# A gated mix of a spectral filter and a state-space filter: ScalarE takes 1-g, GpSimd the gate products, x comes in 16 parts, and the order is new

## The chip, the cores and the metric

The kernel runs on one core of one Trainium2 chip, in one launch, with float32 data. The metric is the device time of that launch in microseconds. The core has five engines that each take their own list of instructions in order: TensorE (PE; its weight loads are listed as PEld), VectorE (DVE), ScalarE (ACT), GpSimd (POOL) and SyncE (SP). They meet through semaphores, and data comes and goes over DMA queues: nearly all transfers are issued by SP, a few by GpSimd.

## The reference, cut to what matters

x is 1 x 2048 x 512 (positions by channels). Two filters of x are mixed by a gate that depends on the position alone:

```python
g = sigmoid((x * gate_w).sum(-1, keepdims=True))
a = irfft2(rfft2(x) * (w_r + 1j * w_i), s=(2048, 512))     # filter A
y = irfft(rfft(x^T, 4096) * rfft(K, 4096), 4096)[:, :, :2048]   # filter B, K[d] = 2 Re sum_n C[d,n] exp(A[d,n] dt[d] l)
b = y^T + x * D_skip
out = g * a + (1 - g) * b
```

## The kernel before, in words

**Filter A** is the two-dimensional transform, written as matmuls of 64 to 128 rows with constant matrices. The transform over 2048 positions has two steps, of 32 and of 64 points; the one over the 512 channels has two halves of 128 points each.

- *Stage 1.* x lies in DRAM in the order in which it is needed and comes in twelve parts, cut at the channels in `_E` (L57); each part is one transfer into VA, which SP issues in a row at the start (L233). The parts go in pairs: C (L248 to 258) multiplies a pair with the matrix s1e, in two halves f, into two PSUM tiles p_s, and c (`c_a`, L264) turns each half, 32 x 32 numbers at a time, by one STREAM_TRANSPOSE of VectorE into AR. When the last pair has gone through, AR holds all of it and VA is free.
- *Units.* The spectrum is cut into nine units (`UNITS`), eight of 128 frequencies and one of 64. Each unit runs through the same chain: P (TensorE, second step over positions, p_t, L411), t (ScalarE copies p_t to et, L416), D (TensorE, over channels, p_d, L425), d and z (ScalarE copies of half of p_d, L432, and of the first row, L444), Z (VectorE, sum and difference in PSUM, L438 and L439), y (ScalarE puts the first row back, L449 and L450), W and U (VectorE, the products with w, L460 to L465, into tw), p (GpSimd, sums of products, px, L472 and L473), g (GpSimd, sum and difference into gt, L484 and L485), h (ScalarE, two small copies for the first row, L491 and L492), I (TensorE, back over channels, p_v, L500), i (ScalarE copies half of p_v to po, L505), V (VectorE, ai, L515), B (TensorE, p_ia, L523 to L526), e (ScalarE copies p_ia to ei, L530), b (SP stores ei to DRAM, L536) and w (SP loads it again into VA in the order of the last step, L539).

**Filter B.** In this data the decay of every channel is so small that K is constant over the 2048 positions within float32, and the long convolution is a running sum times one number for each channel, s0. `N` works on the parameters: N0 takes maxima on VectorE, N1 the exponential of the step size and N3 (`level`) s0; N2 (`small`, L278 to L281) makes an exponential on ScalarE and with it, on GpSimd, the test of each channel; G4 counts the channels that pass and G5 casts the count (L351), which then chooses between the end of the program and a general path (L627), not taken here. A second copy of x with channels on partitions, XT, is loaded in four quarters of 1 MB (X, L299). Each quarter has two halves r of 1024 positions: x scales one into PSUM (ScalarE, L303), m is the running sum v (VectorE scan, L309), and then D_skip times x is added in one of three ways: o and F (ScalarE scales XT, L312, and a DMA issued by GpSimd adds v, L318), o and r (ScalarE, then an add on GpSimd, L315), or k (one VectorE instruction with two inputs from SBUF, L321).

**The gate.** G0 multiplies the four quarters of XT with gate_w (TensorE, p_gate, L336); G1 is the sigmoid (ScalarE, two instructions, L340); G2 makes 1-g in two instructions of VectorE (L343) and copies a piece of it to gc (L345). H spreads g and 1-g over the partitions by way of DRAM: g1 (L362), ga (L369) and gb (L365).

**The end.** M multiplies the last matrix of filter A, s1a, with g (ga, four VectorE instructions, L567); u multiplies XT with 1-g for eight of the 32 blocks of positions (gb, four VectorE instructions, L374). Y turns XT back to positions on partitions, by matmuls with the unit matrix eye (p_y, L549), in eight groups j of four blocks. For six of them s (ScalarE, L554, four instructions each) writes p_y times 1-g into AR, then Q (TensorE, p_oa, L578) makes filter A's share and q (VectorE, L591) adds the two. For the two groups in `DIRECT` Y and Q sum in one PSUM tile and a (ScalarE, L586) copies it. Each group is stored by SP in two transfers (L582).

**What sets the order.** The text PLAN (L41 to L53) is executed word by word: a letter names the function, the number the unit, group, half or part; the sign after `:` is the PSUM tile (four in all), after `/` the block of SBUF (13) and after `.` the short block (3) that it takes. `tc.manual_schedule()` keeps that order on each engine, so that a word stands behind all earlier words of its engine, and a tile can be taken again only when its last reader is done. The word R issues the loads in the list `loads`. The words E put five matmuls each on numbers that nobody reads (L245).

```python
_E = [0, 4, 8, 16, 24, 32, 40, 52, 64, 80, 96, 112, 128]
DIRECT = (0, 1)
LAST = np.array([2 * j + k % 2 + 16 * (k // 2) for j in range(8) for k in range(4)])
UNITS = [8, 0, 1, 2, 3, 4, 5, 6, 7]
```

Of the kernel before, what the change touches and what calls it, by code (L numbers as in the profile page):

```python
# [30 lines left out]
P = 128  # L31
# [25 lines left out]
_E = [0, 4, 8, 16, 24, 32, 40, 52, 64, 80, 96, 112, 128]  # L57
# [112 lines left out]
def body(ctx: ExitStack, tc: tile.TileContext, x, xg, xm, xt, w, wh, prms, vecs, gw, dskip,  # L170
# [57 lines left out]
    with tc.manual_schedule():  # L228
# [48 lines left out]
        def small():  # L277
            S.activation(big[:, 0], big[:, 0], AF.Exp)  # L278
            G.tensor_tensor(sm, big[:, 0], big[:, 1], op=ALU.add)
            G.tensor_tensor(sm, sm, few[:, 0], op=ALU.mult)  # L280
            G.tensor_scalar(sm, sm, float(L), TAU, op0=ALU.mult, op1=ALU.is_le)  # L281
# [49 lines left out]
        def G_(k):  # L331
            if k == 0:
                t_["pg"] = psum("p_gate")
                for i in range(4):
                    for q in range(4):
                        T.matmul(t_["pg"][32 * q:32 * q + 32, 0], gws[:, i], XT[:, i, 512 * q:512 * q + 512], start=i == 0, stop=i == 3, tile_position=(0, 32 * q))  # L336
            elif k == 1:
                t_["gs"] = blk([P, 2, 512], "gs")
                for h, o, g in halves():
                    S.activation(o, g, AF.Sigmoid)  # L340
            elif k == 2:
                for h, o, g in halves():
                    V.tensor_scalar(h, o, -1.0, 1.0, op0=ALU.mult, op1=ALU.add)  # L343
                t_["gc"] = short("gc").rearrange("p i j k -> p (i j k)")[:, 0:128]
                V.tensor_copy(t_["gc"].rearrange("p (c b) -> p c b", b=4), t_["gs"][:, 1].rearrange("p (c b) -> p c b", b=16)[:, :, 0:4])  # L345
            elif k == 4:
                t_["pc"] = psum("p_count")
                for i in range(4):
                    T.matmul(t_["pc"][0:1, 0, 0:1], sm[:, i:i + 1], one, start=i == 0, stop=i == 3)
            else:  # L350
                V.tensor_copy(count, t_["pc"][0:1, 0, 0:1])  # L351
# [20 lines left out]
        def share(i):  # L372
            v = XT[:, i].rearrange("p (c b) -> p c b", b=16)[:, :, 0:4]
            V.tensor_tensor(v, v, t_["gb"], op=ALU.mult)  # L374
# [166 lines left out]

        def Y_(j):
            p = t_["py", j] = psum("p_y").rearrange("p k (b i d) -> p (k b) i d", b=2, i=2)
            xv = XT.rearrange("p (i e) (a g b) -> p i g b (e a)", i=2, g=2, b=32)
            for k in range(4):
                for i in range(2):
                    for g in range(2):
                        first = k % 2 == i == 0 if j in DIRECT else True
                        T.matmul(p[64 * g:64 * g + 64, k, i], xv[:, i, g, LAST[4 * j + k]], eye, start=first, stop=j not in DIRECT, tile_position=(0, 64 * g))  # L549

        def s_a(j):
            for k in range(4):
                b = LAST[4 * j + k]
                S.activation(AR[:, 4 * j + k].rearrange("p (i d) -> p i d", i=2), t_["py", j][:, k], AF.Copy, scale=g1[:, 1, b:b + 1])  # L554
# [8 lines left out]
        def gated(k):  # L563
            w = s1a[k].rearrange("p b (h a) -> p b h a", h=2)
            ga = t_["ga"].rearrange("p a b -> p b a")[:, 16 * k:16 * k + 16]
            for h in range(2):
                V.tensor_tensor(w[:, :, h], w[:, :, h], ga, op=ALU.mult)  # L567
# [26 lines left out]
        def load_prm(k):  # L594
# [14 lines left out]
            lambda: (nc.sync.dma_start(ldt, vecs[:, 0]), load_prm(0)),  # L609
            lambda: (load_prm(1), load_prm(2)),  # L610
# [6 lines left out]
            "B": B_, "e": e_a, "b": b_a, "w": b_b, "Y": Y_, "s": s_a, "S": load_a, "M": gated, "Q": Q_, "q": q_a, "a": a_a, "R": lambda k: loads[k](),  # L617
# [243 lines left out]
```

## Time and profile before

| | |
|---|---|
| runs | 135.46, 135.97 and 136.91 us, median 135.97 |
| profiled execution | 136.17 us, of which the span of the trace is 134.0 |
| mean granted clock of TensorE | 0.948 |
| busy: PE / DVE / ACT / POOL | 114.0 / 97.2 / 71.4 / 50.4 us |
| DMA | 32.66 MB, 244 GB/s on average |

The span runs from the first to the last instruction or transfer that the profiler saw; the device time is 2.2 us longer. A line of the timeline gives the start, the length, the engine, the tile, the line of the kernel, the operation, output and input, how many instructions it holds, and in square brackets the idle time of the engine ahead of it with what ended it. A line of the groups gives the busy time and the mean of one in ns, then the idle time ahead of them and what ended most of it; in a list of single groups the three numbers are the shortest, the mean and the longest in ns. In a table of windows stand the busy time and, in brackets, the number of instructions of PE, PEld, DVE, ACT and POOL, then the clock granted to TensorE (1.00 is full speed), the share of the time in which the DMA engines were busy, and what they moved in GB/s. The chain is the work that ended last, followed back from the end of the span.

### The profile page before, as it was taken

The numbers are of one execution on the slowest core, as the hardware profiler recorded it, in microseconds if no ns is written. First come the engines' busy times: TensorE is split into PE (matmuls) and PEld (weight loads), VectorE is DVE, ScalarE is ACT, GpSimd is POOL, SyncE is SP. The second block draws the span as 40 slices with busy tenths as digits, with TensorE's granted clock in tenths as the row PEclk, the third lists the DMA queues.
The fourth block names the chain that finished last, engine by engine and source line by source line (L and its number), as shares of the span: only waits on it lengthen the run. The fifth ranks groups of instructions, "written<-read, shape, count | busy, mean of one in ns | idle before, by whom it ended". The sixth has DMA issues, their size and how long they took to land.

```text
span 134.0 us, 2683 instructions
## 1 busy us (share of the span) xinstructions
PE 114.0 (85%) x1035; PEld 85.2 (64%) x1035; DVE 97.2 (73%) x103; ACT 71.4 (53%) x136; POOL 50.4 (38%) x49
## 2 busy tenths in 40 slices
PE   6999798899999985698989899999659999999200
PEld 6853234899973974687977349963524999769100
DVE  0196599999999799977698679993789960476200
ACT  3000044489487991849578779865913639604300
POOL 0000000000499994795999289980080000000000
PEclk9999999999999999779999999999986999999955
DMA  3999999998798839463599889797995970199950
GB/s 98 316 329 389 397 340 355 366 417 270 232 346 274 256 87 196 91 195 119 164 264 179 192 284 335 158 373 183 301 323 157 318 157 5 48 380 331 334 191 2
DMA packets 14226, 32.66 MB, mean 244 GB/s; under 512 B 2000, under 2 KB 7420, under 8 KB 13308
## 3 DMA queue, kind: packets, MB, share of 16 engines
q1 hardware_dynamic: 13916, 30.30, 69.7%
q0 software_dynamic: 288, 2.10, 8.3%
q8 instruction: 10, 0.16, 0.5%
q14 instruction: 12, 0.10, 0.2%
HBM read 21.86 MB, written 8.40 MB: 226 GB/s over the span
## 4 chain that ended last, share of the span: by engine, by line
PE 48%; DVE 14%; DMA 13%; ACT 12%; SPq 4%; issue 2%; DVEq 0%; ACTq 0%
PE p_y L549 11%; PE p_t L411 9%; PE p_d L425 8%; DMA VA<-in_x_dram 7%; PE p_ia L526 6%; DMA VA<-ad 6%; DVE AR L264 6%; PE p_v L500 4%; PE p_oa L578 4%; DVE ai L515 3%; SPq L233 3%; DVE gs L343 3%; ACT po L505 2%; ACT XT L312 2%; DVE v L309 2%
## 5 line engine op out<-in xcount | busy, mean ns | idle before, releaser
L411 PE MATMUL p_t<-s2e,AR 128*128 128x128 f32 x136 | 18.0, 290 | 4.2 <-ACT et L416 2.5
L264 DVE STREAM_TRANSPOSE AR<-p_s 128x512 f32<-128x512 f32 (+3 forms) x12 | 15.2, 1357 | 7.7 <-PE p_s L258 7.7
L411 PEld LDWEIGHTS p_t<-s2e,AR 128*128 128x128 f32 x136 | 17.1, 203 | 5.3 <-ACT et L416 2.9
L472 POOL TENSOR_TENSOR px<-tw 128x512 f32<-128x512 f32 (+1 forms) x9 | 11.2, 1248 | 20.3 <-DVE tw L465 20.3
L500 PEld LDWEIGHTS p_v<-dbw,gt 128*128 128x128 f32 x136 | 15.7, 192 | 3.8 <-issue 2.7
L425 PE MATMUL p_d<-et,dfw 128*128 128x256 f32 (+1 forms) x72 | 16.8, 379 | 1.0 <-ACT et L416 0.7
L500 PE MATMUL p_v<-dbw,gt 128*128 128x128 f32 x136 | 16.2, 277 | 1.3 <-issue 1.1
L258 PE MATMUL p_s<-VA,last 64*64 64x256 f32 (+3 forms) x192 | 15.5, 450 | 1.0 <-DMA VA<-in_x_dram 1.0
L549 PEld LDWEIGHTS p_y<-eye,XT 128*64 128x64 f32 x256 | 14.8, 196 | 2.2 <-issue 1.9
L526 PE MATMUL p_ia<-ai,s2p 128*128 128x512 f32 x30 | 15.1, 643 | 1.1 <-DVE ai L515 1.1
L549 PE MATMUL p_y<-eye,XT 128*64 128x128 f32 x256 | 15.5, 282 | 0.0
L425 PEld LDWEIGHTS p_d<-et,dfw 128*128 128x128 f32 x72 | 13.0, 197 | 3.0 <-ACT et L416 1.0
L554 ACT ACTIVATE AR<-p_y,g 128x256 f32<-128x256 f32 x24 | 9.3, 481 | 10.1 <-PE p_y L549 10.1
L515 DVE TENSOR_TENSOR ai<-p_v,po 128x512 f32<-128x512 f32 (+1 forms) x18 | 10.8, 652 | 3.7 <-ACT po L505 3.7
L591 DVE TENSOR_TENSOR AR<-p_oa,AR 128x1024 f32<-128x1024 f32 x6 | 7.1, 1219 | 8.6 <-PE p_oa L578 7.3
L530 ACT COPY ei<-p_ia 128x1024 f32<-128x1024 f32 x8 | 8.1, 1009 | 9.2 <-PE p_ia L526 9.2
L258 PEld LDWEIGHTS p_s<-VA,last 64*64 64x64 f32 x192 | 6.9, 133 | 8.8 <-issue 5.6
L473 POOL TENSOR_TENSOR px<-tw 128x512 f32<-128x512 f32 (+1 forms) x9 | 11.2, 1244 | 1.7 <-DVE tw L463 1.7
L484 POOL TENSOR_TENSOR gt<-px 128x512 f32<-128x512 f32 (+1 forms) x9 | 11.6, 1293 | 0.5
L485 POOL TENSOR_TENSOR gt<-px 128x512 f32<-128x512 f32 (+1 forms) x9 | 11.6, 1294 | 0.0
L309 DVE TENSOR_TENSOR_SCAN v<-pers,v,p_x 128x1024 f32<-128x1024 f32 x4 | 9.4, 2345 | 2.6 <-ACT p_x L303 2.5
L465 DVE TENSOR_TENSOR tw<-p_d,w 128x1024 f32<-128x1024 f32 x8 | 9.7, 1215 | 2.1 <-DMA w<-hT 1.2
(68 smaller groups left out, 155.9 us busy)
## 6 DMA issues: line engine op xcount, KB each, us to landing
XT<-in_xt_dram SPq DMA_DIRECT2D x4, 1024.0 KB
w<-in_w_dram SPq DMA_DIRECT2D x8, 512.0 KB
ad<-ei SPq DMA_DIRECT2D x16, 256.0 KB
VA<-ad SPq DMA_DIRECT2D x8, 512.0 KB
out_dram<-AR SPq DMA_DIRECT2D x16, 256.0 KB
VA<-in_x_dram SPq DMA_DIRECT2D x4, 512.0 KB
XT<-v POOLq DMA_DIRECT2D x2, 1024.0 KB, 8.4
VA<-in_x_dram SPq DMA_DIRECT2D x4, 256.0 KB
```

The lines of the kernel that those rows point to most:

```text
L258: T.matmul(p[f][o:o + 64, h, :n], s1e[r:r + 64, f * u], xv[h][r:r + 64, u], start=u == 0, stop=u == 1, tile_position=(r, o))
L264: V.transpose(ar, t_["c", q][:, :, :32 * n].rearrange("p h (b d) -> p h d b", d=n))
L309: V.tensor_tensor_scan(v, one.broadcast_to([P, 1024]), t_["v1", r], t_["v0", r - 1][:, 1023:1024] if r % 2 else 0.0, op0=ALU.mult, op1=ALU ...
L411: T.matmul(p[:, q, :, 64 * v:64 * v + 64], AR[:, 16 * (q // 2) + sl, 128 * (q % 2):128 * (q % 2) + 128], s2e[:, k], start=True, stop=True)
L425: T.matmul(p[:, o, :, h, :n], dfw[:, 2 * h + o], et[:, ::-1] if h else et, start=True, stop=True)
L472: G.tensor_tensor(po[:, 0], t1[:, :, 0], t1[:, :, 1], op=ALU.add)
L484: G.tensor_tensor(gv[:, :, 0], src[0], src[1], op=ALU.add)
L485: G.tensor_tensor(gv[:, ::-1, 1], src[0], src[1], op=ALU.subtract)
L500: T.matmul(p[:, v, h, o], t_["gt", u][:, o, v, 2 * h:2 * h + 2].rearrange("p c k -> p (c k)"), dbw[:, h, o], start=True, stop=True)
L515: V.tensor_tensor(ai[:, :, :, k], t_["pi", u][:, :n, :, 0], t_["po", u][:, :n], op=ALU.subtract if k else ALU.add)
L526: T.matmul(p[:, v], s2p, t_["ai", pr][:, v], start=True, stop=True)
L549: T.matmul(p[64 * g:64 * g + 64, k, i], xv[:, i, g, LAST[4 * j + k]], eye, start=first, stop=j not in DIRECT, tile_position=(0, 64 * g))
```

## The change

- x comes in 16 parts instead of 12; the eight pairs are of 4, 6, 6, 8, 8, 10, 10 and 12 channels per part.
- 1-g (G2) and the copy gc are made on ScalarE. The exponential of N2 moves into G1, ahead of the sigmoid.
- The products u and M are made on GpSimd.
- Y, for the six groups that are not direct, handles one half i of the channels for eight blocks of positions, not both halves for four: groups 11, 12 and 13 need the first two quarters of XT, 21, 22 and 23 the last two. s takes four of these blocks by four ScalarE instructions of 128 columns; the new word f takes four by one VectorE instruction, with g1 spread over the columns.
- The parameter loads are grouped in another way, and PLAN is new: other units first, other places for E, N, G, X, R, o, F, k, u and M.

Lines after L276 move by 1 to 20: L343 is L344 in the changed kernel, L374 is L375, L549 is L557, L567 is L587, L578 is L598, L591 is L611.

```diff
-_E = [0, 4, 8, 16, 24, 32, 40, 52, 64, 80, 96, 112, 128]
+_E = [0, 4, 8, 14, 20, 26, 32, 40, 48, 56, 64, 74, 84, 94, 104, 116, 128]
...
         def small():
-            S.activation(big[:, 0], big[:, 0], AF.Exp)
             G.tensor_tensor(sm, big[:, 0], big[:, 1], op=ALU.add)
...
             elif k == 1:
+                S.activation(big[:, 0], big[:, 0], AF.Exp)
                 t_["gs"] = blk([P, 2, 512], "gs")
                 for h, o, g in halves():
                     S.activation(o, g, AF.Sigmoid)
             elif k == 2:
                 for h, o, g in halves():
-                    V.tensor_scalar(h, o, -1.0, 1.0, op0=ALU.mult, op1=ALU.add)
+                    S.activation(h, o, AF.Copy, bias=1.0, scale=-1.0)
                 t_["gc"] = short("gc").rearrange("p i j k -> p (i j k)")[:, 0:128]
-                V.tensor_copy(t_["gc"].rearrange("p (c b) -> p c b", b=4), t_["gs"][:, 1].rearrange("p (c b) -> p c b", b=16)[:, :, 0:4])
+                S.copy(t_["gc"].rearrange("p (c b) -> p c b", b=4), t_["gs"][:, 1].rearrange("p (c b) -> p c b", b=16)[:, :, 0:4])
...
         def share(i):
             v = XT[:, i].rearrange("p (c b) -> p c b", b=16)[:, :, 0:4]
-            V.tensor_tensor(v, v, t_["gb"], op=ALU.mult)
+            G.tensor_tensor(v, v, t_["gb"], op=ALU.mult)
...
+            if j in DIRECT:
+                p = t_["py", j] = psum("p_y").rearrange("p k (b i d) -> p (k b) i d", b=2, i=2)
+                todo = [(p[:, k, i], i, k, k % 2 == i == 0) for k in range(4) for i in range(2)]
+            else:
+
+                i, j2 = j // 10 - 1, j % 10
+                p = t_["py", j] = psum("p_y").rearrange("p k (b d) -> p (k b) d", b=4)
+                todo = [(p[:, k], i, k, True) for k in range(8)]
+                j = 2 * j2
+            for o, i, k, first in todo:
+                for g in range(2):
+                    T.matmul(o[64 * g:64 * g + 64], xv[:, i, g, LAST[4 * j + k]], eye, start=first, stop=j not in DIRECT, tile_position=(0, 64 * g))
...
+        def mixed(j, b):
+            i, j2 = j // 10 - 1, j % 10
+            n = 4 * (2 * j2 + b)
+            return AR[:, n:n + 4, 128 * i:128 * i + 128], t_["py", j][:, 4 * b:4 * b + 4], n
+
+        def s_a(j):
+            o, p, n = mixed(j % 100, j // 100)
             for k in range(4):
...
+                b = LAST[n + k]
+                S.activation(o[:, k], p[:, k], AF.Copy, scale=g1[:, 1, b:b + 1])
+
+        def s_b(j):
+            o, p, n = mixed(j % 100, j // 100)
+            gv = g1[:, 1].rearrange("p (h b o) -> p h b o", h=2, o=1)[:, :, n // 2:n // 2 + 2].broadcast_to([P, 2, 2, P])
+            V.tensor_tensor(*(v.rearrange("p (h b) d -> p h b d", h=2) for v in (o, p)), gv, op=ALU.mult)
...
             for h in range(2):
-                V.tensor_tensor(w[:, :, h], w[:, :, h], ga, op=ALU.mult)
+                G.tensor_tensor(w[:, :, h], w[:, :, h], ga, op=ALU.mult)
...
-            lambda: (nc.sync.dma_start(ldt, vecs[:, 0]), load_prm(0)),
-            lambda: (load_prm(1), load_prm(2)),
+            lambda: (load_prm(0), load_prm(1)),
+            lambda: (nc.sync.dma_start(ldt, vecs[:, 0]), load_prm(2)),
```

Of PLAN, which is rewritten as a whole, the end reads as follows before (first) and after the change:

```text
V5/0 B5:3 k6 k7 u1 e5/3 r1 w6 Y4:2 s4 Y6:1 Y2:3 u0 b5 Y3:2 w5 s6 u2 u3 M1 w4 Y5:1 s3 s5 G5 M0 Y0:0 Q0 s2 a0 Q6:2 Q5:1
Q2:3 q6 q5 Q7:0 Q4:2 q2 Q3:1 q3 Y7:3 s7 q4 Y1:1 Q1 q7 a1
```
```text
w6 x6:3 w4 V1/4 b2 s12 V0/0 B1:1 m6 x7:0 m7 b6 Y11:3 r5 b3 w1 w2 e1/3 k7 b1 Y13:1 w5 k6 s11 M1 Y21:0 f21 s112 f121
Y22:2 f122 s13 f22 w0 s113 s111 Y23:1 f23 M0 Q7:3 f123 u0 q7 Q4:0 u2 Q6:2 q4 Q2:1 q2 q6 Q3:3 q3 u3 u1 Q5:0 q5 Y1:1 Q1
a1 Y0:2 Q0 a0
```

**ScalarE around the gate.** Of the instruction list of ScalarE (line, instruction, output and input tiles, shape of one, how often in a row), before, from the D_skip product ahead of the sigmoid on:

```order
L312 ACTIVATE XT<-XT,pers 128x1024
L340 ACT_TABLE_LOAD
L340 ACTIVATE gs<-p_gate 128x16x16
L340 ACTIVATE gs<-p_gate 128x2x8x16
L505 COPY po<-p_v 128x512
```

And after, where last in L338 holds the numbers of N2 and et is the copy of p_t:

```order
L312 ACTIVATE XT<-XT,pers 128x1024 x2
L338 ACTIVATE last<-last 128x4
L341 ACT_TABLE_LOAD
L341 ACTIVATE gs<-p_gate 128x16x16
L341 ACTIVATE gs<-p_gate 128x2x8x16
L445 COPY first<-p_d 1x256
```

Nine copies of units on from the sigmoid, the list after the change goes on:

```order
L450 COPY p_d<-ds 1x2x128
L451 COPY p_d<-first 1x256
L344 ACTIVATE gs<-gs 128x2x8x16 x2
L346 COPY gc<-gs 128x128
L417 COPY et<-p_t 128x1024
```

The exponential stands ahead of the table load of the sigmoid, and the two 1-g and the copy gc have come to ScalarE, in front of a copy of p_t.

**TensorE from the last units to the end.** Before, from the last B groups on:

```order
L526 MATMUL p_ia<-ai,s2p 128x512 x4
L500 MATMUL p_v<-dbw,gt 128x128 x8
L349 MATMUL p_count<-pers,last 1x1 x4
L526 MATMUL p_ia<-ai,s2p 128x512 x2
L549 MATMUL p_y<-eye,XT 64x128 x96
L578 MATMUL p_y<-VA,s1a 64x256 x8
L578 MATMUL p_oa<-VA,s1a 64x256 x48
```

And after:

```order
L527 MATMUL p_ia<-ai,s2p 128x512 x6
L501 MATMUL p_v<-dbw,gt 128x128 x12
L350 MATMUL p_count<-pers,last 1x1 x4
L557 MATMUL p_y<-eye,XT 64x128 x16
L524 MATMUL p_ia<-ai,s2e 128x512
L525 MATMUL p_ia<-ai,s2e 128x512
L527 MATMUL p_ia<-ai,s2p 128x512
L557 MATMUL p_y<-eye,XT 64x128 x80
L598 MATMUL p_oa<-VA,s1a 64x256 x48
```

One group of sixteen p_y has moved ahead of the last p_ia; the other five follow it, and the products p_oa begin behind all six. The ten matmuls on p_idle, five and five before (the second five among the last units), stand together right behind the last p_s.

**VectorE and GpSimd at the end.** VectorE before, from the last ai on:

```order
L515 TENSOR_TENSOR ai<-p_v,po 128x4x128 x2
L321 SCALAR_TENSOR_TENSOR XT<-XT,pers,v 128x1024 x2
L374 TENSOR_TENSOR XT<-XT,gb 128x128x4 x4
L567 TENSOR_TENSOR s1a<-s1a,ga 128x16x32 x2
L351 CAST count<-p_count 1x1
L567 TENSOR_TENSOR s1a<-s1a,ga 128x16x32 x2
L591 TENSOR_TENSOR AR<-p_oa,AR 128x1024 x6
```

After (the SCALAR_TENSOR_TENSOR into v are the scans L309):

```order
L516 TENSOR_TENSOR ai<-p_v,po 128x2x128 x2
L309 SCALAR_TENSOR_TENSOR v<-pers,p_x 128x1024
L309 SCALAR_TENSOR_TENSOR v<-pers,v,p_x 128x1024
L321 SCALAR_TENSOR_TENSOR XT<-XT,pers,v 128x1024 x2
L574 TENSOR_TENSOR AR<-p_y,g_62 128x4x128 x6
L611 TENSOR_TENSOR AR<-p_oa,AR 128x1024 x6
```

And GpSimd after the change, from the last gt on:

```order
L485 TENSOR_TENSOR gt<-px 128x2x4x64
L486 TENSOR_TENSOR gt<-px 128x2x4x64
L315 TENSOR_TENSOR XT<-XT,v 128x1024 x2
L587 TENSOR_TENSOR s1a<-s1a,ga 128x16x32 x4
L375 TENSOR_TENSOR XT<-XT,gb 128x128x4 x4
L647 TENSOR_LOAD count
```

The eight products have left VectorE for the end of GpSimd's list, behind both adds L315; on VectorE the last two scans now stand behind the last ai, and six evacuations of p_y (L574) are new.

36 lines of the change are left out of this document (14 added, 22 removed).

## The prediction

> **What bounds the kernel now.** I read the page first: TensorE holds 48% of the chain that ended last, more than three times any other engine, so the question is where TensorE waits, and for whom.
>
> ```profile
> span 134.0 us, 2683 instructions
> ...
> PE 48%; DVE 14%; DMA 13%; ACT 12%; SPq 4%; issue 2%; DVEq 0%; ACTq 0%
> ```
>
> Then the windows, cut at the places where TensorE stops (columns: window, length, busy time of PE, PEld, DVE, ACT, POOL with counts, granted clock, DMA share, GB/s):
>
> ```profile
> 0.00:24.00 24.00, 20.85 (x224) 11.92 (x224) 15.45 (x18) 4.85 (x13) 0.60 (x6) 1.00 0.91 318
> 24.00:42.00 18.00, 18.00 (x128) 14.97 (x132) 17.78 (x15) 12.50 (x23) 6.51 (x6) 1.00 0.91 329
> 42.00:54.70 12.70, 9.65 (x76) 7.89 (x68) 11.71 (x15) 9.43 (x18) 9.92 (x9) 1.00 0.75 185
> 54.70:75.00 20.30, 18.56 (x109) 15.86 (x110) 16.54 (x22) 14.45 (x30) 18.11 (x17) 0.92 0.64 163
> 75.00:99.10 24.10, 21.13 (x116) 14.16 (x117) 18.49 (x20) 17.95 (x29) 13.90 (x13) 1.00 1.00 284
> 99.10:113.80 14.70, 14.70 (x200) 12.01 (x200) 10.16 (x11) 7.47 (x18) 1.37 (x1) 0.88 0.60 157
> ```
>
> The reader is to see three stages. Up to 24 us VectorE turns x and sets the end. From 24 to 125 TensorE is short of full by 3.05 + 1.74 + 2.97 = 7.76 us, and its clock is below 1 in two windows. After 125 only stores run, and no edit touches them: the 9.1 us from the last matmul to the end of the span stay. The profiled execution took 136.17 us, near the median of 135.97, and I subtract from 136.17.
>
> **The front: x in 16 parts.** The timeline of VectorE and the chain:
>
> ```profile
> 5.67 0.63 DVE L264 STREAM_TRANSPOSE AR<-p_s 128x256 f32<-128x256 f32 x1 [4.67 <-PE p_s L258]
> 6.97 4.17 DVE L264 STREAM_TRANSPOSE AR<-p_s 128x512 f32<-128x512 f32 x5 [0.67 <-PE p_s L258]
> 12.16 2.84 DVE L264 STREAM_TRANSPOSE AR<-p_s 128x768 f32<-128x768 f32 x2 [1.02 <-PE p_s L258]
> 4.94 4.56 PE L258 MATMUL p_s<-VA,last 64*64 64x128 f32 x96
> ```
> ```profile
> 14.38 1.96 PE p_s L258 x14
> ...
> 16.37 5.59 DVE AR L264 x3
> ```
>
> A transpose of 1024 columns takes 5.59/3 = 1.86 us in a row of them, one of 768 takes 2.84/2 = 1.42: 1.82 ns a column at both sizes, so sixteen small transposes cost VectorE what twelve do. What can go are its gaps: 0.67, 1.02 and, between 15.00 and 16.37, 1.37, each the time in which a part lands and TensorE does its half of the pair (1.96 us for the large ones). With parts of 640 and 768 instead of 768 and 1024 columns the later two, 2.39 together, should close. The order now turns the second half of the first pair first, which starts VectorE later by half of that pair's matmuls: the row of 4.94 holds pairs of 128, 256 and 256 columns, so the first takes 0.91 and its half 0.46. **Term 1: -1.9**; the ends are 0 (the parts land in the same lump) and -3.05 (no gap at all).
>
> **1-g on ScalarE.** The chain, then VectorE's line, the same place on GpSimd and on TensorE, and the window of 3.5 us:
>
> ```profile
> 48.35 3.70 DVE gs L343 x2
> ...
> 53.69 1.00 ACT et L416
> ```
> ```profile
> L343 DVE TENSOR_SCALAR gs<-gs x2: 284/1930/3576, 48.3 to 48.5; 128x256 f32<-128x256 f32 x2
> ```
> ```profile
> 48.33 1.03 POOL L318 DMA_DIRECT2D XT<-v  x1 [0.27 <-ACT p_d L449]
> ...
> 50.38 1.50 POOL L485 TENSOR_TENSOR gt<-px 128x512 f32<-128x512 f32 x1
> ```
> ```profile
> 50.36 1.89 PE L425 MATMUL p_d<-et,dfw 128*128 128x256 f32 x8
> 54.74 3.27 PE L411 MATMUL p_t<-s2e,AR 128*128 128x128 f32 x16 [2.49 <-ACT et L416]
> 57.80 2.37 PE L425 MATMUL p_d<-et,dfw 128*128 128x256 f32 x8
> 60.00 1.95 PE L411 MATMUL p_t<-s2e,AR 128*128 128x128 f32 x16
> ```
> ```profile
> 54.70:58.20 3.50, 3.46 (x17) 3.40 (x18) 3.37 (x8) 2.97 (x7) 3.42 (x4) 0.59 0.21 34
> ```
>
> Of two equal L343 one takes 0.284 us and the other 3.576, ending at 52.04, just after GpSimd's run of 48.33 to 51.88: it waited for GpSimd. Behind it stand gc, the sums L438 and L439, ScalarE's L449 and L416, and then TensorE, idle for 2.49 us; behind that idle time the clock falls to 0.59 for 3.5 us, so that sixteen p_t take 3.27 instead of 1.95 and eight p_d 2.37 instead of 1.89. On ScalarE there is no such wait in any row; its nearest rows are the sigmoids over the same shape:
>
> ```profile
> L340 ACT ACTIVATE gs<-p_gate 128x256 f32<-128x256 f32 x2 | 0.7, 381 | 0.0
> ```
>
> Two of them and a small copy come to about 1.0 us, in front of one p_t copy, which TensorE can cover with the p_d and p_v that now stand before it. **Term 2: -(2.49 + 1.32 + 0.48) = -4.3**; if ScalarE's 1.0 is then the last to end, -3.3.
>
> **Exponential and order, 75 to 103 us.** The timeline of ScalarE, GpSimd and TensorE:
>
> ```profile
> 86.22 1.27 POOL L485 TENSOR_TENSOR gt<-px 128x512 f32<-128x512 f32 x1
> 94.05 0.39 ACT L491 COPY gt<-px 1x256 f32<-1x256 f32 x1
> 95.66 1.28 ACT L278 ACT_TABLE_LOAD   x1
> ```
> ```profile
> 89.05 1.28 PE L245 MATMUL p_idle<-last 128*128 128x128 f32 x10
> 90.17 3.60 PE L526 MATMUL p_ia<-ai,s2p 128*128 128x512 f32 x8
> 99.10 3.16 PE L526 MATMUL p_ia<-ai,s2p 128*128 128x512 f32 x4 [0.66 <-DVE ai L515]
> 102.19 11.63 PE L549 MATMUL p_y<-eye,XT 128*64 128x128 f32 x192
> ```
>
> The last gt is ready at 87.49, but ScalarE reaches its two fix-ups at 94.05, then loads a table (1.28) before the copy of p_v, and TensorE waits. In the changed order the exponential stands before the sigmoid's load, while the first table is still in, so a load is saved; the last unit's p_v comes with no load between; sixteen p_y, whose quarters are done by then, go in front of the last p_ia; and the filler matmuls are at the front, behind the transposes. Idle time 2.97, filler 1.28 and the half clock at 99.10 (3.16 against 3.60/2 = 1.80) make 5.6. **Term 3: -5.6**; the other end is 0, if the order brings other waits in their place.
>
> **What is late next: the last quarter.** Now TensorE has all of p_y behind it; afterwards the three p_y groups of the channels' second half wait for the last scans and L321, with only one p_ia group and two p_y to cover them.
>
> ```profile
> L321 DVE SCALAR_TENSOR_TENSOR XT<-XT,pers,v x2: 1272/1976/2680, 98.9 to 101.5; 128x1024 f32<-128x1024 f32 x2
> ```
> ```profile
> 98.13 2.34 POOL L315 TENSOR_TENSOR XT<-XT,v 128x1024 f32<-128x1024 f32 x1
> L309 DVE TENSOR_TENSOR_SCAN v<-pers,v,p_x 128x1024 f32<-128x1024 f32 x4 | 9.4, 2345 | 2.6 <-ACT p_x L303 2.5
> L472 POOL TENSOR_TENSOR px<-tw 128x512 f32<-128x512 f32 x8 | 10.5, 1313 | 20.3 <-DVE tw L465 20.3
> L567 DVE TENSOR_TENSOR s1a<-s1a,ga 128x512 f32<-128x512 f32 x4 | 4.2, 1091 | 0.0
> L374 DVE TENSOR_TENSOR XT<-XT,gb 128x512 f32<-128x512 f32 x4 | 2.5, 679 | 0.0
> ```
>
> After the last ai VectorE has two scans (2 x 2.35) and two L321 (2 x 1.27 alone, plus 1.4 for one that meets GpSimd, as 2.68 against 1.272 shows): 8.6. TensorE has the last p_ia group, three matmuls in six records, 2.7 (eight take 3.60), and two p_y groups of the six in the row of 102.19, 3.9: together 6.6. With 0.4 for the steps between, **term 4: +2.4**. At the lower end it is 0. The upper end comes from the eight gate products now on GpSimd, a train that L321 meets. Their price is not in the trace: between 1.31 (L472, 512 columns) and 2.07 (the same times 1.6, as the strided L567 stands to the plain L374). I take 1.31: L472 too reads pieces of a larger tile, and the products are nearest to it in engine and size. From the end of the second L315 to the free start of L321 I count 9.2 us (three L515, 2.0, two scans, 4.7, a wait of about 1.1 for p_v, and the 1.4 above); six products stand in that stretch, 7.9 at 1.31, which hides, or 12.4 at 2.07, which adds 3.2: upper end +5.6.
>
> The Trainium skill, page SBUF — State Buffer, section Who interferes with whom, says that a VectorE instruction with two SBUF inputs and a GpSimd instruction that reads SBUF block each other, the one issued first finishing first. The trace agrees with the blocking (2.68 against 1.272). By that rule both L321 would wait for a GpSimd product each, 2 x 1.3 in place of 1.4, and the sum would be 128.7.
>
> **The rest.** The gate's matmuls now stand behind four p_t and three p_d, 22.1 + 4 x 1.95 + 3 x 1.89 = 35.6 us; the last x quarter has 11.6 MB ahead of and in it (4.2 of x, 4.2 of the quarters, 1.05 of w, 0.9 of s2e, 0.8 of prm, 0.4 of small ones), at the 320 GB/s of the first two windows 36.3 us: **term 5: +0.7** (0 to 2). Taking p_y out of PSUM was 24 activations of 481 ns; it becomes 24 of half the width on ScalarE (between half of 481 and all of it) and six on VectorE (near 0.68, as L515, which reads PSUM and SBUF too), which lost 6.7 us of products: they lie beside 11.6 us of p_y. Uncovered, the last group of four would cost up to 4 x 0.48 = 1.9 us.
>
> ```profile
> L554 ACT ACTIVATE AR<-p_y,g 128x256 f32<-128x256 f32 x24 | 9.3, 481 | 10.1 <-PE p_y L549 10.1
> L515 DVE TENSOR_TENSOR ai<-p_v,po 128x512 f32<-128x512 f32 x16 | 10.2, 681 | 3.7 <-ACT po L505 3.7
> ```
>
> Sum: -1.9 - 4.3 - 5.6 + 2.4 + 0.7 = -8.7, so **127.5 us**.
>
> **Rivals.** (A) The order gives back term 3: other in-order waits stand where these stood. For it: GpSimd's gate chain is 18.11 busy of 20.3 in 54.7 to 75, so it soon binds again. Against it: it also starts sooner. 136.17 - 1.9 - 4.3 + 2.4 + 0.7 = 133.1. (B) Nearly every wait goes: 7.76 idle, 1.80 + 1.36 of slow clock, 1.28 filler, 1.9 in front: 122.1. For it: the reordering names each; against: in-order queues seldom lose all. (C) The GpSimd train decides: extra time 6p - 9.2 for a price p each. It makes the kernel slower than before from p = 3.2 us; at 3.5 us, 139.3. For it: L343 waited through three GpSimd instructions. Against it: a GpSimd product of 512 columns takes 1.31, and 1.50 at 50.38, during a transfer that GpSimd issued. (D) The change does not do what it says: parts land in one lump, ScalarE's 1-g stalls the p_t as VectorE's did, and new waits take the rest: about 136.
>
> **How the numbers follow.** Chances: forecast 0.50, A 0.22, B 0.15, C 0.09, D 0.04. The range takes in B's edge and A and the bounds of terms 1 and 4: 122.5 to 134.0, leaving out C, D and a little of B. A measurement tells about 1% (1.4 us) from no change: faster 0.87 (forecast, A, B), same 0.04 (D), slower 0.09 (C).
>
> **What would show it.** Term 1: the first p_t starts near 22.1. Term 2: no L343 kind on VectorE, no TensorE idle over 1 us near 50, clock 1. Term 3: two table loads, not three; TensorE idle below 2 us between the middle and the first p_y. Term 4: a wait of TensorE for XT of L321's kind, 2 to 3 us; if it is over 5, the train is the cause. The forecast is wrong if the last matmul lies outside 113 to 122.

## The result, and the profile after

The changed kernel takes 126.09 us in the median of four runs (125.29 to 126.51), against 135.72 us of the kernel before in the runs beside it: the ratio is 0.927, with a 95% interval of 0.919 to 0.934. Run again later beside other kernels it took 126.96 us against 134.63, a ratio of 0.943 (0.937 to 0.950). The two agree on 5 to 8% less; what the intervals leave between them is taken up in the last section. Medians and ranges here are of all executions, while the ratios with their intervals compare only those executions of either kernel that lie within 1.5% of its fastest, so that a median and a ratio need not agree. The profiled execution took 125.29 us, with a span of 123.2.

The page of the changed kernel, its span and its chain by engine:

```profile
span 123.2 us, 2834 instructions
...
PE 63%; DMA 11%; DVE 8%; SPq 6%; ACT 4%; issue 2%; DVEq 0%
```

TensorE's share of the chain has risen from 48% to 63%: less of the end is set by anyone else. The windows of the changed kernel, cut at the first p_t, at 42, 55, 75 and 87.3 us, and at TensorE's last stop (columns as in the windows before):

```profile
0.00:22.98 22.98, 21.58 (x296) 17.25 (x297) 16.25 (x22) 4.92 (x12) 0.60 (x6) 1.00 0.90 326
22.98:42.00 19.02, 17.64 (x129) 13.58 (x128) 18.16 (x16) 14.27 (x23) 7.70 (x7) 1.00 0.87 327
42.00:55.00 13.00, 13.00 (x90) 11.55 (x89) 10.44 (x12) 11.48 (x26) 11.46 (x10) 1.00 0.88 230
55.00:75.00 20.00, 19.57 (x124) 15.74 (x123) 17.10 (x25) 15.82 (x34) 18.75 (x19) 1.00 0.90 236
75.00:87.30 12.30, 12.07 (x76) 8.92 (x76) 8.19 (x9) 9.68 (x16) 12.14 (x11) 1.00 0.95 289
87.30:97.97 10.67, 8.70 (x105) 6.69 (x103) 10.01 (x9) 8.36 (x23) 8.31 (x7) 1.00 0.96 266
97.97:115.20 17.23, 17.14 (x288) 13.94 (x288) 10.75 (x12) 2.56 (x8) 2.45 (x2) 1.00 0.57 192
```

From the first p_t to the last matmul TensorE is short of full by 1.38 + 0 + 0.43 + 0.23 + 1.97 + 0.09 = 4.1 us, where it was 7.76, and the clock is 1.00 in all of these windows, where it was 0.92 and 0.88 in two. GpSimd is the busiest engine beside it now: 18.75 of 20.0 us and 12.14 of 12.3. The two stops that are left, in TensorE's timeline, and the last scans and L321 on VectorE:

```profile
22.98 3.74 PE L412 MATMUL p_t<-s2e,AR 128*128 128x128 f32 x32
...
38.82 1.92 PE L336 MATMUL p_gate<-XT,gws 128*32 128x512 f32 x16 [1.38 <-DMA XT<-in_xt_dram]
...
97.97 5.72 PE L557 MATMUL p_y<-eye,XT 128*64 128x128 f32 x96 [1.98 <-DVE XT L321]
```
```profile
89.70 2.28 DVE L309 TENSOR_TENSOR_SCAN v<-pers,p_x 128x1024 f32<-128x1024 f32 x1
92.08 2.35 DVE L309 TENSOR_TENSOR_SCAN v<-pers,v,p_x 128x1024 f32<-128x1024 f32 x1
94.46 3.37 DVE L321 SCALAR_TENSOR_TENSOR XT<-XT,pers,v 128x1024 f32<-128x1024 f32 x2
```

These are the waits of terms 5 and 4, at 1.38 and 1.98 us. Ahead of the second stand VectorE's two scans and two L321, one after the other without a gap.

### The profile page after: what moved, and what is told of

Read it like the earlier page. It is cut to its first block, busy times and chain, and to the rows that moved or that the text cites. A ratio compares the mean times of both kernels' runs of the same rounds, so it can differ in the third digit from the quotient of the medians.

```text
span 123.2 us, 2834 instructions
## 1 busy us (share of the span) xinstructions
PE 109.7 (89%) x1099; PEld 87.7 (71%) x1099; DVE 90.9 (74%) x102; ACT 68.1 (55%) x138; POOL 61.4 (50%) x57
## 4 chain that ended last, share of the span: by engine, by line
PE 63%; DMA 11%; DVE 8%; SPq 6%; ACT 4%; issue 2%; DVEq 0%
PE p_v L501 13%; PE p_d L426 9%; PE p_t L412 9%; PE p_ia L527 8%; PE p_y L557 8%; PE p_s L259 6%; DMA XT<-in_xt_dram 6%; DMA VA<-in_x_dram 6%; PE p_oa L598 4%; SPq L234 4%; DVE v L309 4%; DVE XT L321 3%; PE p_idle L246 2%; PE p_y L598 2%; PE p_gate L336 2%
## 5 line engine op out<-in xcount | busy, mean ns | idle before, releaser
L265 DVE STREAM_TRANSPOSE AR<-p_s 128x384 f32<-128x384 f32 (+4 forms) x16 | 15.4, 1059 | 5.8 <-PE p_s L259 5.8
L473 POOL TENSOR_TENSOR px<-tw 128x512 f32<-128x512 f32 (+1 forms) x9 | 10.9, 1215 | 16.4 <-DVE tw L466 14.8
L557 PE MATMUL p_y<-eye,XT 128*64 128x128 f32 x256 | 15.9, 281 | 2.0 <-DVE XT L321 2.0
L557 PEld LDWEIGHTS p_y<-eye,XT 128*64 128x64 f32 x256 | 15.0, 197 | 3.7 <-issue 2.9
L412 PE MATMUL p_t<-s2e,AR 128*128 128x128 f32 x136 | 16.0, 275 | 0.0
L412 PEld LDWEIGHTS p_t<-s2e,AR 128*128 128x128 f32 x136 | 15.7, 192 | 0.2
L259 PE MATMUL p_s<-VA,last 64*64 64x256 f32 (+4 forms) x256 | 14.9, 378 | 0.3 <-DMA VA<-in_x_dram 0.3
L527 PE MATMUL p_ia<-ai,s2p 128*128 128x512 f32 x30 | 13.9, 592 | 0.0
L259 PEld LDWEIGHTS p_s<-VA,last 64*64 64x64 f32 x256 | 10.8, 133 | 3.8 <-DMA VA<-in_x_dram 1.1
L466 DVE TENSOR_TENSOR tw<-p_d,w 128x1024 f32<-128x1024 f32 x8 | 9.7, 1216 | 2.0 <-ACT p_d L451 1.2
L486 POOL TENSOR_TENSOR gt<-px 128x512 f32<-128x512 f32 (+1 forms) x9 | 11.1, 1237 | 0.0
L474 POOL TENSOR_TENSOR px<-tw 128x512 f32<-128x512 f32 (+1 forms) x9 | 10.9, 1215 | 0.0
L464 DVE TENSOR_TENSOR tw<-p_d,w 128x1024 f32<-128x1024 f32 x8 | 9.7, 1217 | 0.9 <-ACT p_d L451 0.9
L417 ACT COPY et<-p_t 128x1024 f32<-128x1024 f32 (+1 forms) x9 | 8.6, 959 | 2.9 <-PE p_t L412 2.9
L303 ACT ACTIVATE p_x<-XT,pers 128x1024 f32<-128x1024 f32 x8 | 8.9, 1120 | 2.2 <-DVE AR L265 1.4
L606 ACT COPY AR<-p_y 128x1024 f32<-128x1024 f32 x2 | 2.0, 1013 | 14.7 <-PE p_y L598 14.7
```

The costliest lines, as they stand in the source:

```text
L259: T.matmul(p[f][o:o + 64, h, :n], s1e[r:r + 64, f * u], xv[h][r:r + 64, u], start=u == 0, stop=u == 1, tile_position=(r, o))
L265: V.transpose(ar, t_["c", q][:, :, :32 * n].rearrange("p h (b d) -> p h d b", d=n))
L412: T.matmul(p[:, q, :, 64 * v:64 * v + 64], AR[:, 16 * (q // 2) + sl, 128 * (q % 2):128 * (q % 2) + 128], s2e[:, k], start=True, stop=True)
L473: G.tensor_tensor(po[:, 0], t1[:, :, 0], t1[:, :, 1], op=ALU.add)
L474: G.tensor_tensor(po[:, 1, :, ::-1], t2[:, :, 0], t2[:, :, 1], op=ALU.subtract)
L486: G.tensor_tensor(gv[:, ::-1, 1], src[0], src[1], op=ALU.subtract)
```

## The experiments

**One part undone in the changed kernel.** First 1-g and gc back on VectorE:

```diff
-                    S.activation(h, o, AF.Copy, bias=1.0, scale=-1.0)
+                    V.tensor_scalar(h, o, -1.0, 1.0, op0=ALU.mult, op1=ALU.add)
...
-                S.copy(t_["gc"]...
+                V.tensor_copy(t_["gc"]...
```

> The changed kernel with one part undone: 1-g and the copy gc are made on VectorE again, at the same place of the order. If VectorE's wait for GpSimd is what 1-g cost (the theory of the prediction), one of the two instructions waits 2 to 4 us again while GpSimd works back to back, the products of that unit come as much later, and the kernel takes 1 to 4 us more than the changed one (127 to 130). If the new order has taken 1-g off the path anyway (the rival), the time stays within 0.7 us of the changed kernel, whatever the instruction itself shows.

Measured: 128.88 us (127.39 to 129.42), ratio 0.958 (0.937 to 0.978). VectorE's timeline and TensorE's:

```profile
47.30 1.80 DVE L344 TENSOR_SCALAR gs<-gs 128x256 f32<-128x256 f32 x2
49.13 1.25 DVE L346 COPY gc<-gs 128x128 f32<-128x128 f32 x1
```
```profile
52.70 1.99 PE L426 MATMUL p_d<-et,dfw 128*128 128x256 f32 x8 [1.09 <-DVE tw L464]
55.27 1.96 PE L527 MATMUL p_ia<-ai,s2p 128*128 128x512 f32 x4 [0.58 <-ACT p_d L451]
```

The three small instructions hold VectorE for 3.05 us beside a busy GpSimd, where ScalarE takes 0.72 + 0.30 in the changed kernel. TensorE waits 1.09 and 0.58 us that were not there, and reaches the last p_y 2.25 us later (100.22). That bears out the theory, with about 2.2 us of trace; the median is 2.8 us above that of the first runs of the changed kernel and 1.9 above that of the later ones.

The eight products back on VectorE:

```diff
-            G.tensor_tensor(v, v, t_["gb"], op=ALU.mult)
+            V.tensor_tensor(v, v, t_["gb"], op=ALU.mult)
...
-                G.tensor_tensor(w[:, :, h], w[:, :, h], ga, op=ALU.mult)
+                V.tensor_tensor(w[:, :, h], w[:, :, h], ga, op=ALU.mult)
```

> The changed kernel with the eight gate products on VectorE again, in the same order. VectorE then has 4 x 1.09 + 4 x 0.68 = 7.1 us more behind L321, ahead of and between the evacuations of p_y. If their move to GpSimd is needed for the new end of the order, the evacuations come late, TensorE waits for PSUM tiles, and the time rises by 3 to 6 us. If the products lie beside TensorE's p_y in either place, it stays within 1 us. In both, L321 should take 1.27 twice, since no GpSimd product stands beside it.

Measured: 133.39 us (130.42 to 134.50), ratio 0.980 (0.965 to 0.995), the dearest of the four to undo. TensorE's last rows:

```profile
97.94 5.73 PE L557 MATMUL p_y<-eye,XT 128*64 128x128 f32 x96 [1.09 <-DVE XT L321]
106.38 6.96 PE L598 MATMUL p_oa<-VA,s1a 64*64 64x256 f32 x96 [2.71 <-DVE s1a L587]
116.51 3.56 PE L557 MATMUL p_y<-eye,XT 128*64 128x128 f32 x32 [3.17 <-DVE XT L375]
```

As expected, L321 now takes 1.28 us twice, and the wait in front of p_y is down to 1.09. But the products stand in VectorE's row ahead of and between the evacuations L574 and the sums L611, and TensorE waits 2.71 and 3.17 us for them. These waits come to 5.0 us more than in the changed kernel (2.71 + 3.17, less the 0.89 saved in front of p_y). In the new order the move to GpSimd is needed.

x in the twelve parts of before, in the changed order (`_E` as before, and two pairs fewer in PLAN):

> The changed kernel with x in the twelve parts of before, in the changed order. If the finer parts give the earlier start, the first p_t moves from 22.98 back towards 24 us and the time rises by 1.0 (what the two traces differ by) to 1.9 us (term 1 of the prediction). If the later p_t is given back because GpSimd's chain or the load of the last quarter binds later, the time rises by less than 0.5 us.

Measured: 125.36 us (124.98 to 127.33), ratio 0.936 (0.919 to 0.954), no slower than the changed kernel. In the trace the first p_t stands at 23.85 and TensorE's last stop ends at 99.00, so 0.9 and 1.0 us later than in the changed kernel; the last matmul ends 1.0 us later too, but the span is 0.3 us longer only. That is less than it seems, since this start moves from execution to execution: in the nine traces with sixteen parts, in either order, the first p_t stands at 22.63 to 23.94 (median 22.99), in the five with twelve at 23.20 to 23.98 (median 23.41). The finer parts bring some 0.4 us to TensorE, and no gain in the time could be measured.

The exponential back in N2, which stands among the units:

```diff
         def small():
+            S.activation(big[:, 0], big[:, 0], AF.Exp)
...
-                S.activation(big[:, 0], big[:, 0], AF.Exp)
```

> The changed kernel with the exponential back in N2, which now stands among the units near 61 us, so that ScalarE loads a table three times. If the load is what stalled TensorE in the kernel before, it costs up to 1.3 us here too, since ScalarE is 15.8 of 20.0 us busy there. If only its place at the last unit made it dear, the units in flight cover it and the time rises by less than 0.5 us.

Measured: 128.00 us (127.59 to 128.67), ratio 0.957 (0.944 to 0.971), so 1.0 to 1.9 us above the two medians of the changed kernel: about the larger of the two expectations or more. ScalarE's and GpSimd's timelines:

```profile
64.38 1.28 ACT L279 ACT_TABLE_LOAD   x1
```
```profile
61.25 1.28 POOL L486 TENSOR_TENSOR gt<-px 128x512 f32<-128x512 f32 x1
65.96 0.20 POOL L280 TENSOR_TENSOR last<-last 128x4 f32<-128x4 f32 x1 [3.43 <-ACT last L279]
```

The load costs here by way of GpSimd, not by ScalarE's own copies coming late. GpSimd's three tiny instructions of N2 stand in the middle of its row of unit work and wait 3.43 us for the exponential: 1.85 until ScalarE has reached it (62.53 to 64.38), 1.28 for the load and the rest for the exponential. TensorE then waits 1.28 us for gt L486, which it does not in the changed kernel. Not all of the loss in the trace is from there: x was turned 1 us later in this execution (first p_t at 23.94).

**One part alone in the kernel before.** 1-g and gc on ScalarE (the first diff, the other way round):

> The kernel before with one change alone: 1-g and gc on ScalarE, at the same place of the order. The prediction's term 2 says 3.3 to 4.3 us less (131.7 to 132.7 in place of 136): no wait of VectorE for GpSimd near 48 us, TensorE's idle time of 2.49 us gone and its clock at 1 near 55 us. The rival, that the old order gives it back at the next in-order wait, says less than 1.5 us.

Measured: 133.19 us (131.65 to 134.31), ratio 0.984 (0.968 to 1.000). TensorE's timeline:

```profile
51.47 1.99 PE L425 MATMUL p_d<-et,dfw 128*128 128x256 f32 x8 [0.49 <-ACT et L416]
58.54 2.05 PE L411 MATMUL p_t<-s2e,AR 128*128 128x128 f32 x16 [1.57 <-DVE tw L460]
```

The wait of 2.49 us is gone, and so is the half clock behind it, but 1.57 us come back one unit later, where p_t waits for VectorE's products L460 to free its tile (L460 itself had waited 1.27 us for a transfer into w). About half of term 2 is left by the ratio, 2.2 us, but the interval reaches 1.000. The traces allow a closer look. From the p_t behind the wait of 0.59 us to the p_v behind that of 0.23 us TensorE takes 19.65 us here (48.96 to 68.61). With 1-g on VectorE it takes 22.24 in the kernel before (48.50 to 70.74), where the clock fell behind the wait, and 20.61 in the run with the products alone, below (47.87 to 68.48), where it stayed at 1.00. So about 1.0 us is the wait and 1.6 the clock.

x in sixteen parts (`_E` as after the change, two pairs more in PLAN):

> The kernel before with x in sixteen parts alone. The prediction's term 1 says 1.9 us earlier at the first p_t, near 22.1, and as much at the end. What the changed kernel showed (22.98) says 1.0. If the old order gives it back at the waits of 42 to 75 us, the end moves by less than 0.5 us.

Measured: 135.57 us (133.69 to 137.77), ratio 1.000 (0.993 to 1.008). The timeline says why so little comes of it:

```profile
23.48 3.81 PE L411 MATMUL p_t<-s2e,AR 128*128 128x128 f32 x32 [0.78 <-DMA s2e<-in_c_s2e_dram]
```

The first p_t now waits for a constant that SP issues behind the transfers of x, four more of which are ahead of it.

The exponential ahead of the sigmoid:

> The kernel before with the exponential alone moved ahead of the sigmoid's table load. One table load of 1.28 us goes; ScalarE reached it at 95.66 with TensorE waiting behind (idle 1.07, 1.24 and 0.66 us from 94 to 99, then the clock below 1). If the load is what TensorE waited for, 1.3 to 3 us go. If ScalarE's late arrival at 94.05 is the cause and the load only stood behind it, less than 1.3 us go.

Measured: 134.33 us (133.60 to 135.78), ratio 1.004 (0.998 to 1.010). No table load is left at the end, and ScalarE and TensorE show what it was worth:

```profile
96.16 0.59 ACT L505 COPY po<-p_v 128x512 f32<-128x512 f32 x1 [1.25 <-PE p_v L500]
```
```profile
94.10 2.02 PE L500 MATMUL p_v<-dbw,gt 128*128 128x128 f32 x16 [1.07 <-issue]
98.21 1.95 PE L526 MATMUL p_ia<-ai,s2p 128*128 128x512 f32 x4 [1.82 <-DVE ai L515]
```

ScalarE now waits 1.25 us for p_v, in the time in which it loaded the table before. TensorE's waits of 1.24 and 0.66 have become one of 1.82, so its idle time has not gone. What did change in the trace is the clock behind it: the last four p_ia take 1.95 us, where they took 3.16. In the 3.5 us from their start the granted clock is 1.00 in both traces of the old order with the early exponential, and 0.51 to 0.70 in the four without it. Whether that is the edit or chance is open; the ratio shows no gain.

The late exponential also holds up GpSimd in the kernel before, as its timeline shows:

```profile
97.24 0.20 POOL L279 TENSOR_TENSOR last<-last 128x4 f32<-128x4 f32 x1 [7.43 <-ACT last L278]
```

Its last add L315 stands behind these, starts at 98.13 and meets L321. With the early exponential the add is done before, and L321 takes 1.28 us twice.

The products on GpSimd (the second diff, the other way round):

> The kernel before with the eight gate products alone on GpSimd, where they follow its last add. Prediction and rival differ in L321: by the blocking seen in the trace it takes up to 2.7 us each beside GpSimd. VectorE has nothing else to do there but these products, and p_y covers 11.6 us: the time should stay within 1 us. A rise by over 2 us would mean that products on GpSimd cost far more than the 1.5 us each of the changed kernel.

Measured: 136.65 us (134.91 to 137.45), ratio 1.019 (1.007 to 1.031). The two L321 and the products:

```profile
L321 DVE SCALAR_TENSOR_TENSOR XT<-XT,pers,v x2: 1683/2521/3359, 96.5 to 98.1; 128x1024 f32<-128x1024 f32 x2
```
```profile
L567 POOL TENSOR_TENSOR s1a<-s1a,ga 128x512 f32<-128x512 f32 x4 | 6.4, 1626 | 0.0
L374 POOL TENSOR_TENSOR XT<-XT,gb 128x512 f32<-128x512 f32 x4 | 5.8, 1483 | 0.2 <-issue 0.2
```

L321 takes 2.52 us each on average instead of 1.98, and GpSimd's products are 1.5 to 2.2 times as long as VectorE's (1.09 and 0.68). The first L321 is held by a product, the second by the late add L315. In the old order the move costs 1.4 us by the medians and 2.5 by the ratio, more than the 1 us expected. All four single edits in the old order together would come to about zero.

**All edits in the old order, and two mends,** on one chip with the changed kernel. The changed kernel itself:

> The changed kernel unchanged, as the measure for the runs beside it on one chip: 126.1 us, 125.3 to 126.6, by its earlier runs.

Measured: 126.96 us (126.42 to 129.38). The four edits in the order of before:

> All the edits (1-g on ScalarE, exponential ahead of the sigmoid, products on GpSimd, x in sixteen parts) in the order of before, without the new p_y groups. Alone the edits gave about -2.2, +0.5, +2.5 and 0 us in that order. If they only add, 136 less 0 to 1.5; then the order is worth 8 to 9 us and only with the edits. If the sum of the prediction's terms held without the order, 127.5 to 130.

Measured: 131.42 us (130.95 to 132.58), ratio 0.977 (0.971 to 0.983): 3.2 us less than before, more than the sum of the single ones. The order, with its new p_y groups, is worth the other 126.96 - 131.42 = -4.5 us. With the exponential early, GpSimd's add and products no longer meet L321 (1278 ns each in this run), and the granted clock is 1.00 in every window up to 120 us.

One half of the last quarter taken from L321 to ScalarE and GpSimd:

```diff
- ... m6 x7:0 m7 b6 ... Y13:1 w5 k6 s11 M1 Y21:0 ...
+ ... m6 x7:0 o6 m7 b6 ... Y13:1 w5 s11 M1 r6 Y21:0 ...
```

> The changed kernel with one half of the last quarter taken from VectorE's L321 to ScalarE (L312) and GpSimd (L315), behind the first two products M. If VectorE's row of two scans and two L321 is what p_y waits 1.98 us for (term 4), the wait falls below 0.5 us and the time by 1 to 2 us (124.1 to 125.1). If GpSimd's train of products is the cause, it gets 2.35 us longer, L321 waits longer, and the time rises by up to 2 us.

Measured: 125.33 us (124.57 to 126.12), 1.6 less than the changed kernel beside it. TensorE's timeline:

```profile
96.30 5.72 PE L557 MATMUL p_y<-eye,XT 128*64 128x128 f32 x96 [0.39 <-DVE XT L321]
103.34 5.41 PE L598 MATMUL p_oa<-VA,s1a 64*64 64x256 f32 x96 [1.32 <-POOL XT L375]
```

The wait is 0.39 us: VectorE's row was what p_y waited for, not GpSimd's train, which is 2.4 us longer here. p_y starts 1.67 us earlier than in the first trace of the changed kernel, but p_oa only 0.28 (103.34 for 103.62). The profile puts the new wait of p_oa to L375, but p_oa reads nothing that L375 writes. The list of instructions of L598 has a wait of TensorE for semaphores that begins at 100.7 and takes 2328 ns:

```profile
L598 PEldq EVENT_SEMAPHORE  x6: 51/51/2328, 100.7 to 104.7; - x6
```

In the trace the semaphore that ends it, at 103.03, is that of the last load into VA (the word w, L540), which SP issued at 97.45. In the changed kernel this load landed at 102.16, while p_y still ran. So this load is the next bound, and the time saved in front of p_y is mostly given back to it. Most of the 1.6 us between the medians is then probably the clock, which can fall behind a stop of 1.98 us (last section): the 96 p_y take 5.72 us here and 7.32 in the trace of the changed kernel beside it.

In addition a p_d group ahead of the gate's matmuls:

```diff
-... G0:3 p4/9 Z7 N0 y7 W7/a l5 o0 o1 G1/b D5:0 ...
+... D5:0 G0:3 p4/9 Z7 N0 y7 W7/a l5 o0 o1 G1/b ...
```

> As the run before, and in addition one p_d group of TensorE goes in front of the gate's matmuls, so that the wait of 1.38 us for the last quarter of x is covered by 1.7 us of work (term 5). If TensorE is the bound there, 1.4 us more go: 122.7 to 123.7 in all. If GpSimd's chain (over 90% busy from 42 to 87 us) binds instead, the wait turns up again behind it and less than 0.5 us goes.

Measured: 124.81 us (123.97 to 126.18), ratio 0.926 (0.920 to 0.932) on the chip where the changed kernel has 0.943. The wait for the last quarter is gone, and TensorE stops elsewhere:

```profile
45.47 1.99 PE L426 MATMUL p_d<-et,dfw 128*128 128x256 f32 x8 [0.27 <-ACT et L417]
47.79 2.02 PE L501 MATMUL p_v<-dbw,gt 128*128 128x128 f32 x16 [0.32 <-POOL px L473]
```

The last row of p_y begins at 96.46, as without the swap (96.30). GpSimd, 18.5 of 20.0 us busy between 55 and 75 us, gives the pace there, as the second theory said; the 0.5 us between the medians is within their spread. This is the fastest kernel of all here, 2.2 us under the changed one in the median.

## Why the prediction was right or wrong

The time and the direction were right: 127.5 us predicted, 126.1 and 127.0 measured, inside the range. The last matmul ends at 115.1, inside the 113 to 122 that were set. But the sum was better than its terms. In the traces the front gave 0.9 us less than forecast, while the idle time fell by 1.3 us more (the waits between 55 and 75 us, which no term names) and the tail by 1.0 us; that such errors cancel in part is luck.

**Term 1 (-1.9) was too large.** VectorE's gaps did close, from 0.67, 1.02 and 1.37 to 0.21 and 0.17:

```profile
6.38 1.09 DVE L265 STREAM_TRANSPOSE AR<-p_s 128x256 f32<-128x256 f32 x2 [5.37 <-PE p_s L259]
7.68 1.52 DVE L265 STREAM_TRANSPOSE AR<-p_s 128x384 f32<-128x384 f32 x2 [0.21 <-PE p_s L259]
9.37 11.29 DVE L265 STREAM_TRANSPOSE AR<-p_s 128x384 f32<-128x384 f32 x11 [0.17 <-PE p_s L259]
```
```profile
20.32 2.82 PE L246 MATMUL p_idle<-last 128*128 128x128 f32 x20
```

But VectorE began 0.71 us later (6.38 for 5.67, and I had 0.46), and the ten fillers on TensorE end at 23.14, after the last transpose (21.07 + 1.52 = 22.59): my "behind the transposes" placed them wrongly, as they stand ahead of the first p_t. The first p_t came at 22.98 in place of 22.1, 1.0 us earlier than in the trace before. Over all traces the medians differ by 0.4 us only, and the runs with twelve and sixteen parts show that none of it can be measured at the end.

**Term 2 (-4.3) had the right mechanism.** VectorE's 1-g waits for GpSimd and ScalarE's does not: 0.72 us for both, in one p_t's shadow. The size depends on the order. In the old one about 1.0 us of wait is left, since p_t then waits for L460; in the new one undoing it costs 2.2 us of trace. Of the 4.3, 1.8 was the half clock, which does not come in every run (last section).

**Term 3 (-5.6) had the right size for a partly wrong reason.** The step that failed is that "a load is saved" and that TensorE waited for it: the load of 1.28 us lay beside p_v's 2 us, as the run with the exponential alone shows, where 2.89 us of idle time remain of 2.97. What removed that idle time is the rest of that term, the order. With all edits in the old order TensorE still stops for 1.07 and 1.82 us there and spends 1.28 on filler; in the new order it goes from 75.14 to 96.0 us without a stop, through the last p_v, p_ia and the first p_y. The order as a whole is worth 4.5 us, and that includes the waits of 0.2 to 1.6 us in the middle which it removes and the 1.98 us of term 4 which it adds. The early exponential matters in the new order, through GpSimd, which would wait 3.43 us for it.

**Term 4 (+2.4) was right** in place and cause: the wait is 1.98 us. What it costs is less where the clock holds, since p_oa behind it came only 0.28 us earlier without it. Of two L321 only the first met a GpSimd product (2172 ns against 1274):

```profile
L321 DVE SCALAR_TENSOR_TENSOR XT<-XT,pers,v x2: 1274/1723/2172, 94.5 to 96.6; 128x1024 f32<-128x1024 f32 x2
...
  POOL XT L375: 2.4, 1
```
```profile
93.05 2.50 POOL L375 TENSOR_TENSOR XT<-XT,gb 128x512 f32<-128x512 f32 x2
97.91 2.51 POOL L375 TENSOR_TENSOR XT<-XT,gb 128x512 f32<-128x512 f32 x2 [2.36 <-DVE XT L321]
```

The second could not meet one, because GpSimd's next product needs the quarter that L321 writes, and stood waiting for 2.36 us. So the extra was 0.90 us, not 1.4. The Trainium skill (SBUF — State Buffer, Who interferes with whom) says that the one issued first keeps the other out until it ends. The second of the two products in the row of 93.05 was there first and ended at 95.55, L321 came at 94.46 and took 0.90 us more; in the run with the products alone both L321 were held. The trace agrees with the rule to 0.2 us, since 1.09 us of the product were left. Of the two waits in the 128.7 that I gave for it only one came, by the data dependence, not by the rule.

**Term 5 (+0.7)** measured 1.38 us (1.4 to 1.8 in the runs). The run with the swap shows that it was hardly on the path: GpSimd's chain sets the pace behind it, and the last p_y came no earlier.

**The rivals.** Rival A was not the end, but it is what 1-g and the exponential met alone in the old order: the wait removed gave its time to the next. Rival B did not come either: 4.1 of the 7.76 us of idle time are left. Rival C did not come: the products cost 1.55 and 1.28 us, under the 3.2 from which it decides. What I did not price is the reverse: left on VectorE in the new order, they would have cost 5 us of waits. The tail, which I held at 9.1 us, became 123.2 - 115.1 = 8.1; no run here tells why. Of the 10.9 us between the two profiled executions 10.2 can be placed: 3.7 of idle time (7.76 less 4.1), 3.2 of slow clock, 1.3 of filler among the last units, 1.0 in front and 1.0 in the tail. These are the differences of two executions; the clock and the front differ between executions of one kernel too.

## What to carry to other kernels

In a kernel whose queues are run in order, a single edit is worth what the next wait behind it lets through: here four edits alone gave -2, 0, 0 and +2 us, together -3, and with an order made for them -8 to -10. Before a table load or a busy engine is blamed, look what the engine that waits for it would have waited for anyway. A tiny instruction with a late input, put in the middle of the fullest queue, stops that queue: GpSimd's three 0.2 us instructions kept it idle for 3.43 us, and TensorE waited 1.28 of it. And a removed wait is worth what the next start shows, not its own length: of 1.6 us in front of p_y 0.28 reached p_oa.

## What the runs showed of the hardware that I had not expected

**The clock after a short stop is a matter of chance.** Windows of the changed kernel (first) and of its repeat, behind the same wait of TensorE of 1.98 us, and TensorE's timeline of the repeat:

```profile
98.00:101.50 3.50, 3.50 (x62) 3.50 (x64) 1.29 (x2) 1.49 (x6) 2.42 (x2) 1.00 0.66 157
```
```profile
98.70:102.20 3.50, 3.46 (x40) 3.49 (x42) 0.53 (x1) 1.55 (x7) 2.46 (x2) 0.66 0.64 157
102.20:105.70 3.50, 3.50 (x58) 3.50 (x56) 2.05 (x4) 0.00 (x0) 0.00 (x0) 0.86 0.01 2
```
```profile
98.74 7.32 PE L557 MATMUL p_y<-eye,XT 128*64 128x128 f32 x96 [1.98 <-DVE XT L321]
```

The clock stays at 1.00 in one and falls to 0.66 and 0.86 in the other, where the same p_y take 7.32 us instead of 5.72. The same holds behind the wait of 2.50 us, with the exponential alone (first) and with the products alone in the old order:

```profile
54.00:57.50 3.50, 3.44 (x19) 3.27 (x20) 3.37 (x8) 2.97 (x8) 3.42 (x4) 0.69 0.16 33
```
```profile
54.00:57.50 3.50, 3.38 (x23) 3.22 (x24) 3.37 (x7) 2.97 (x8) 3.42 (x3) 1.00 0.20 31
```

So a stop of 2 to 2.5 us costs itself, or itself and 1.6 to 1.8 us more, and this is enough to explain why the ratio was 0.927 in one set of runs and 0.943 in the other, though that was not shown. The Trainium skill (TensorE: Matmul & The Clock Gate, Part 1) puts the fall after an idle window of some 3.4 us that runs freely. The chance would fit a free-running window, but the fall came here behind stops of 2 us, so the measurement differs from the page there.

**A copy of VectorE with one input is held by GpSimd too, as 1-g is.** The two 1-g and the copy gc, with one input from SBUF, took 522, 1357 and 1245 ns in the first experiment, where one 1-g took 284 and gc 227 in the kernel before. Each ended within 0.2 us behind the end of a GpSimd product (47.67, 48.95 and 50.30). The Trainium skill, in the same section of SBUF — State Buffer, names copies and tensor_scalar among the instructions that can take the ports shared with GpSimd, and the runs agree; ScalarE's 0.72 us for both 1-g, at the same place beside the same GpSimd, agrees with its rule that ScalarE waits for nobody.
